# The maxima product of key tile 1 moved to the head of a pair's first slot, in a fused attention, MLP and soft-MoE kernel

## The chip, the cores and the metric

The kernel runs on one NeuronCore of a Trainium2 chip. The metric is the device time of one execution in microseconds (us). The engines are named as in the profile: PE is TensorE (matmuls; PEld is its weight load), DVE is VectorE, ACT is ScalarE, POOL is GpSimd, SP is SyncE, which issues the DMAs.

## The reference

```python
# q, k, v: (4 batches, 12 heads, 448, 64)
scores = scale * np.matmul(q, k.transpose(0, 1, 3, 2))   # causal mask: -1e9 above the diagonal
scores = scores - np.max(scores, axis=-1, keepdims=True)
attn = np.exp(scores)
attn = attn / (np.sum(attn, axis=-1, keepdims=True) + 1e-09)
x = np.matmul(attn, v)                       # heads joined: (1792, 768)
h = x @ w_in; x = np.maximum(0.01 * h, h) @ w_out        # 768 -> 2048 -> 768
logits = x @ phi                             # 32 slots, 4 for each of 8 experts
d = softmax(logits, axis=0); slot_input = d.T @ x
slot_out[e] = np.maximum(slot_input[e] @ w1[e], 0) @ w2[e]
out = softmax(logits, axis=1) @ slot_out
```

All inputs are float32 and the result is (1792, 768) float32.

## The kernel before

**Pairs and rounds.** Attention works on pairs of heads, 6 pairs for each of the 4 batches, 24 in all. The generator `attention_slots` issues their work in rounds. A round has three slots, each ended by a `yield`. The first loop (L553) serves the first batch. The second loop (L587) holds the rounds n = 7 to 24 and is the one that changes; "round n" below is its loop variable. A round works on three pairs at once: it finishes pair n-1, computes the weights of pair n, and the row maxima of pair n+1.

**Maxima.** A pair's 448 keys and queries are four tiles of 112. For a softmax the row maximum of the scores is wanted first. `maxima(n, tiles)` (L377) multiplies the high parts of q and k of a tile into a PSUM tile `S`, for both heads, and DVE reduces each half to a column of `mxe` (L396, shown as `junk<-S`, followed by a short read of the accumulator). The tiles come in three calls: `TILES[0]` is tile 3 (448 columns, S_3 below), `TILES[1]` tiles 0 and 2 (S_0), `TILES[2]` tile 1 (224 columns, S_1). `lowering(n)` (L402) transposes `mxe` on PE (`mps`), and ACT writes four rows `mr` from it.

**Weights.** `weights(n, g)` (L410) makes the transposed scores in a PSUM tile `T` by six matmuls from the stacks `qkt` and two that add `mr`; T_0, T_1, T_2 are its three calls. ACT takes the exponential into `P`, POOL masks the diagonal blocks (L436) and sums over key tiles into `tsum` (L441, L445).

**End of a pair.** `attend` (L451) multiplies P with v into `O`; `inverses` (L462) makes the row sums `dn`, which ACT copies to `rs` and DVE inverts in two halves (L474, 1.5 us each); `columns` (L486) multiplies O by `rs` and splits the result into two float16 halves, `x16`.

**What fills the slots.** In the rounds of the second loop `stage` (L803) puts a column block of the next product, H = x @ w_in (18 matmuls of 128x448 in float16), after most slots, and `prep_step` puts pieces of the conversion of w_in and w_out (the 64 bit pattern arithmetic on DVE and POOL, `cv`, `cs`, `raw`; w_ps, wt_ps, wp_ps, wf_ps on PE) between them. No H follows the slots 6 and 15 of a batch (`GAPS`), which are the first slots of rounds 9, 12, 15, 18 and 21, 24. H has one PSUM buffer.

**What sets the order.** `in_order` chains all of these matmuls, so PE takes them in the order in which they are written; ACT's order is chained in the same way from the second batch on. DVE's and POOL's order comes from the scheduler. S and T share one PSUM tag, "S", with two buffers of two banks each: a new S or T tile takes a buffer whose last reader (DVE's maxima or ACT's exponential) is done. Which of the two buffers it takes is settled when the program is built, by the scheduler's estimate of what is free first.

Of the kernel before, what the change touches and what calls it, by code (L numbers as in the profile page):

```python
# [34 lines left out]
def tile_attn_moe_softmoe(ctx: ExitStack, tc: tile.TileContext, q, k, v, w_in, w_out, phi, w1, w2, out, dbg=None):  # L35
# [292 lines left out]
    def load_qk(n):  # L328
        b, hp = divmod(n, NP)
        t = att.tile([CP, 2, 2 * NI * D], F32, tag="qk", bufs=2, name=f"qk{n}")  # L330
        t = t.rearrange("p j (c x) -> p j c x", c=NI)
        for j, src in enumerate((q, k)):
            for a in range(2):
                nc.sync.dma_start(
                    t[:, j, :, D * a : D * (a + 1)], src[b, 2 * hp + a].rearrange("(c p) d -> p c d", p=CP)
                )
        qk_t[n] = t
        loaded_last()
# [11 lines left out]
    def reduce_v(n):  # L350

        b, hp = divmod(n, NP)
        if hp == 0:
            v_am[b] = am = const.tile([128, NP + 1], F32, tag="v_am", bufs=2, name=f"v_am{b}")
            nc.vector.memset(am, 0.0)
        with tc.issue_after(last_on(mybir.EngineType.DVE)) if b else ExitStack():
            nc.vector.tensor_reduce(v_am[b][:CP, hp : hp + 1], v_t[n], AX.XY, ALU.max, apply_absolute_value=True)

    def v_scale(b):

        am = v_am[b]
        nc.vector.tensor_reduce(am[:, NP:], am[:, :NP], AX.X, ALU.max)
        s_v[b], inv_v[b] = pow2_scale(am[:, NP:], f"v{b}")

    def qk_stacks(n):

        t = qk_t.pop(n)
        st = att.tile([128, 2, 2, S], F32R, tag="qs", bufs=2, name=f"qkt{n}")
        for j in range(2):
            p = ps_tr(f"qkps{n}_{j}", (128, S))  # L370
            for c in range(NI):
                tr(p[:, CP * c : CP * (c + 1)], t[:, j, c], ident[:CP, :CP])
            scalar.copy(st[:, j, 0], p)
            nc.vector.tensor_tensor(st[:, j, 1], p, st[:, j, 0].bitcast(F32), ALU.subtract)  # L374
        st_t[n] = st

    def maxima(n, tiles):  # L377

        st = st_t[n]
        ps = psum.tile([CP, 2, 512], F32, tag="S", bufs=2, name=f"S{n}_{tiles[0]}")  # L380
        at = 0
        for i in tiles:
            w = CP * (i + 1)
            for a in range(2):
                r = slice(64 * a, 64 * a + 64)
                mm(
                    ps[:, a, at : at + w], st[r, 0, 0, CP * i : w], st[r, 1, 0, :w], start=True, stop=True,
                    skip_group_check=True,
                )
            at += w  # L390
        at = 0
        for i in tiles:
            w = CP * (i + 1)
            for a in range(2):
                junk = att.tile([CP, S], BF16, tag="junk", bufs=1, name=f"junk{n}_{i}_{a}")
                nc.vector.tensor_tensor_reduce(  # L396
                    out=junk[:, :w], in0=ps[:, a, at : at + w], in1=mask[:, S - w :], scale=-1.0, scalar=3e38,
                    op0=ALU.add, op1=ALU.min, accum_out=mxe[n % 2][:, 64 * a + i : 64 * a + i + 1],
                )
            at += w  # L400

    def lowering(n):  # L402

        ps = ps_tr(f"mps{n}", (128, CP))
        tr(ps, mxe[n % 2], ident[:CP, :CP])
        mr_t[n] = mr = att.tile([128, NI, CP], F32R, tag="mr", bufs=1, name=f"mr{n}")
        for i in range(NI):
            scalar.activation(mr[:, i], ps, AF.Copy, scale=own[:, i : i + 1])
# [42 lines left out]
    def attend(n):  # L451

        p, vt = pbuf[n % 2], v_t.pop(n)
        o_t[n] = o = psum.tile([128, S], F32, tag="O", name=f"O{n}")
        for j in range(NI):
            for a in range(2):
                mm(
                    o[64 * a : 64 * a + 64, CP * j :], vt[:, a * NI + j, :], p[j // 2][:CP, a, j % 2, : S - CP * j],
                    start=j == 0, stop=j == NI - 1, skip_group_check=True,
                )  # L460
# [80 lines left out]
    def attention_slots():  # L541


        for n in range(2):
            qk_stacks(n)
            load_qk(n + 2)
            if n == 0:
                for tiles in TILES:
                    maxima(0, tiles)
        for x in range(NP):  # L550
            reduce_v(x)
        v_scale(0)
        for n in range(NP + 1):  # L553
            here, more = n < NPAIR, n + 1 < NPAIR
            if n > 0:
                attend(n - 1)
            if here:
                lowering(n)
            if more:
                maxima(n + 1, TILES[0])  # L560
            if here:
                weights(n, 0)
            yield
            if n > 0:
                inverses(n - 1)
            if more:
                maxima(n + 1, TILES[1])
            if here:
                weights(n, 1)
            yield  # L570
            if n > 0:
                columns(n - 1)
            if here:
                weights(n, 2)
            if more:
                maxima(n + 1, TILES[2])
            if n + 2 < NPAIR:
                qk_stacks(n + 2)
                if n + 4 < NPAIR:
                    load_qk(n + 4)  # L580
            if n + NP < NPAIR:
                load_v(n + NP)
            if NP <= n + NP - 1 < NPAIR:
                reduce_v(n + NP - 1)
            yield

        for n in range(NP + 1, NPAIR + 1):  # L587
            here, more = n < NPAIR, n + 1 < NPAIR
            attend(n - 1)
            inverses(n - 1)  # L590
            if here:
                lowering(n)
            yield
            if more:
                maxima(n + 1, TILES[2])
            if here:
                weights(n, 0)
            if more:
                maxima(n + 1, TILES[0])
            if n % NP == 1 and n + NP - 2 < NPAIR:  # L600
                v_scale(n // NP)
            yield
            if here:
                weights(n, 1)
                weights(n, 2)
            if more:
                maxima(n + 1, TILES[1])
            if n + 2 < NPAIR:
                qk_stacks(n + 2)
                if n + 4 < NPAIR:  # L610
                    load_qk(n + 4)
            if n + NP < NPAIR:
                load_v(n + NP)
            columns(n - 1)
            if n + NP - 1 < NPAIR:
                reduce_v(n + NP - 1)
            yield

    TILES = ((3,), (0, 2), (1,))
    slots_of_attention = attention_slots()  # L620


# [490 lines left out]
```

## Time and profile before

| what | value |
|---|---|
| median of 3 runs | 681.62 us (679.66 to 689.91) |
| the profiled execution | 681.57 us, span 679.8 us |
| mean granted PE clock | 0.963 |
| busy over the span | PE 583.1 us (86%), DVE 362.9 us (53%), ACT 291.9 us (43%), POOL 235.1 us (35%) |
| rounds 7 to 24 | about 103 to 460 us of the span |

The span is the time from the first to the last instruction of the profiled execution; the 1.8 us beside it lie around the instructions. A busy share says how long an engine had work in it. Whether that work sets the time is seen from what the engines wait for: the profile gives, for an instruction, the idle time of its engine just before it and who ended that idle time. Matmuls are pipelined, so a row's duration on PE is longer than the distance to the next row's start.

### The profile page before, as it was taken

The page shows a single profiled execution, that of the slowest core. Times are in us where ns is not written, and L with a number is a line of the kernel's source. Part 1 is how long each engine was busy: PE and PEld are TensorE (multiplying, and loading weights), DVE is VectorE, ACT ScalarE, POOL GpSimd, SP SyncE. Part 2 cuts the span into 40 slices and gives each one's busy share as a digit, 9 for nine tenths or more (in the row PEclk, how much of TensorE's full clock was granted, in tenths as well). Part 3 has the DMA queues.
Part 4 walks back from the last instruction along what each step waited for, and adds up shares of the span by engine and source line. Part 5 has one row for each costly group of instructions (what it writes and reads, how often), then busy time and mean ns, then how long its engine had stood idle before and what let it go on. Part 6 is the DMA issues. An engine that isn't in the chain of part 4 may idle for free.

```text
span 679.8 us, 12302 instructions
## 1 busy us (share of the span) xinstructions
PE 583.1 (86%) x4836; PEld 329.7 (48%) x4836; DVE 362.9 (53%) x884; ACT 291.9 (43%) x571; POOL 235.1 (35%) x247
## 2 busy tenths in 40 slices
PE   3778888989998998999999989999889978997374
PEld 2555555545554555555556544554334434553124
DVE  5868567979855565555557556434664341001004
ACT  2577555767764656564455444531202121011003
POOL 4277862577774335533334422430000000000000
PEclk9999889999999999999999979999999997999958
DMA  9941345556622456543243313029966545999957
GB/s 186 275 110 45 79 133 156 168 161 169 195 70 71 151 179 202 162 132 80 65 127 107 101 40 99 22 65 324 336 279 277 185 171 239 423 425 423 426 216 324
DMA packets 102449, 125.67 MB, mean 185 GB/s; under 512 B 69240, under 2 KB 91256, under 8 KB 98296
## 3 DMA queue, kind: packets, MB, share of 16 engines
q1 hardware_dynamic: 102392, 124.89, 55.9%
q8 instruction: 38, 0.62, 0.4%
q14 instruction: 19, 0.16, 0.1%
HBM read 105.74 MB, written 19.14 MB: 184 GB/s over the span
## 4 chain that ended last, share of the span: by engine, by line
PE 54%; POOL 11%; DMA 11%; DVE 10%; ACT 6%; issue 4%; SPq 2%; ACTq 0%; DVEq 0%; POOLq 0%
PE H L102 25%; DMA w<-in_moe_w_dram 9%; PE O L102 4%; PE T L102 4%; PE g_acc L102 3%; DVE g_nat L632 3%; PE S L102 3%; DVE rs L474 2%; POOL w L245 2%; POOL tsum L445 2%; ACT P L113 2%; POOL tsum L441 2%; PE dn L102 2%; DMA raw_i_None<-in_moe_w_in_dram 2%; POOL P L436 2%
## 5 line engine op out<-in xcount | busy, mean ns | idle before, releaser
L102 PE MATMUL H<-x,w 128*128 128x448 f16 x1152 | 233.5, 357 | 0.7 <-ACT g L113 0.7
L102 PEld LDWEIGHTS <-w 128*128 128x128 f16 x1152 | 112.0, 100 | 112.4 <-issue 21.0
L396 DVE CUSTOM_DVE_ANT_0 junk<-S,mask 112x224 bf16<-112x224 f32 (+3 forms) x192 | 85.0, 443 | 65.0 <-PE S L102 62.1
L113 ACT ACTIVATE g<-H,iv 128x448 f32<-128x448 f32 x58 | 36.8, 635 | 119.8 <-PE H L102 91.4
L474 DVE RECIPROCAL rs<-rs 128x224 f32<-128x224 f32 x36 | 53.4, 1524 | 50.2 <-ACT rs L113 50.2
L113 ACT ACTIVATE P<-T 112x672 f32<-112x672 f32 (+1 forms) x72 | 57.1, 793 | 23.6 <-PE T L102 22.2
L436 POOL TENSOR_SCALAR_AFFINE_SELECT P<-P 112x448 f32<-112x448 f32 x48 | 29.4, 613 | 107.4 <-ACT P L113 76.9
L102 PE MATMUL T<-qkt 64*112 64x336 f32 (+3 forms) x576 | 58.3, 315 | 4.0 <-ACT P L113 3.4
L102 PE MATMUL O<-P,v 112*64 112x448 f32 (+3 forms) x384 | 52.8, 415 | 5.6 <-POOL P L436 4.4
L102 PE MATMUL S<-qkt 64*112 64x224 f32 (+3 forms) x192 | 33.4, 388 | 20.1 <-DVE mxe L396 12.3
L445 POOL TENSOR_TENSOR tsum<-tsum,P 112x448 f32<-112x448 f32 (+1 forms) x48 | 47.6, 993 | 1.9
L102 PEld LDWEIGHTS T<-qkt 64*112 64x112 f32 x576 | 43.1, 180 | 10.2 <-ACT P L113 3.7
L1059 PE MATMUL po<-w,hz 128*32 128x384 f32 x256 | 27.9, 558 | 18.7 <-DMA w<-in_moe_w_dram 18.7
L102 PEld LDWEIGHTS O<-P,v 112*64 112x64 f32 x384 | 25.8, 139 | 31.9 <-issue 14.1
L441 POOL TENSOR_TENSOR tsum<-P 112x672 f32<-112x672 f32 x24 | 39.9, 1663 | 1.9
L963 POOL MEMSET hz<- 128x256 f32 x2 | 0.6, 312 | 108.6 <-PE g_acc L102 108.6
L632 DVE STREAM_TRANSPOSE g_nat<-g 128x448 f32<-128x448 f32 x26 | 16.5, 640 | 34.2 <-ACT g L113 34.2
L374 DVE TENSOR_TENSOR qkt<-qkps,qkt 128x448 fp32r<-128x448 f32 x48 | 29.2, 621 | 9.8 <-ACT qkt L113 9.8
L102 PE MATMUL T<-mr,onesr 64*112 64x448 f32 (+1 forms) x192 | 30.5, 314 | 3.9 <-ACT mr L113 3.9
L102 PEld LDWEIGHTS S<-qkt 64*112 64x112 f32 x192 | 15.9, 182 | 35.1 <-DVE mxe L396 17.5
L113 ACT ACTIVATE mr<-mps,own 128x112 fp32r<-128x112 f32 x96 | 26.2, 361 | 14.5 <-PE mps L102 14.4
L236 POOL TENSOR_TENSOR cv_i_None<-cv_i_None,cs_i_None 128x768 f32<-128x768 f32 x16 | 28.6, 1785 | 11.1 <-ACT cs_i_None L113 11.1
(174 smaller groups left out, 866.8 us busy)
## 6 DMA issues: line engine op xcount, KB each, us to landing
w<-in_moe_w_dram SPq DMA_DIRECT2D x32, 1536.0 KB
raw_i_None<-in_moe_w_in_dram SPq DMA_DIRECT2D x16, 768.0 KB
raw_o_None<-in_moe_w_out_dram SPq DMA_DIRECT2D x10, 768.0 KB
g_far<-g SPq DMA_DIRECT2D x32, 224.0 KB
gb<-g_far SPq DMA_DIRECT2D x8, 896.0 KB
wo<-wsc SPq DMA_DIRECT2D x4, 1536.0 KB
qk<-in_q_dram SPq DMA_DIRECT2D x48, 112.0 KB
qk<-in_k_dram SPq DMA_DIRECT2D x48, 112.0 KB
```

Of the source, the lines that this page charges most:

```text
L102: op(*args, **kwargs)
L113: op(*args, **kwargs)
L236: nc.gpsimd.tensor_tensor(t, t, sg, ALU.mult)
L245: nc.gpsimd.tensor_tensor(lo, w, hi, ALU.subtract)
L374: nc.vector.tensor_tensor(st[:, j, 1], p, st[:, j, 0].bitcast(F32), ALU.subtract)
L396: nc.vector.tensor_tensor_reduce(out=junk[:, :w], in0=ps[:, a, at : at + w], in1=mask[:, S - w :], scale=-1.0, scalar=3e38, op0=ALU.add, o ...
L436: nc.gpsimd.affine_select(out=d, in_=d, compare_op=ALU.is_ge, fill=0.0, base=0, pattern=[[0, 4], [1, CP]], channel_multiplier=-1,)
L441: nc.gpsimd.tensor_tensor(tsum[:CP], p[0][:CP, :, 0, CP:], p[0][:CP, :, 1, : S - CP], ALU.add)
L445: nc.gpsimd.tensor_tensor(y, y, p[1][:CP, :, j, : S - CP * (j + 2)], ALU.add)
L474: nc.vector.reciprocal(rs[:, c : c + S // 2], rs[:, c : c + S // 2])
L632: nc.vector.transpose(g_nat[:, :, 32 * f : 32 * (f + n)].rearrange("p c (f x) -> p f c x", x=32), gts[b, f].rearrange("p (c x) -> p c x", ...
L1059: nc.tensor.matmul(po[h][32 * g : 32 * g + 32], hp[:, (t0 + t) % 8], wt[:, t, DH * h - c0 : DH * (h + 1) - c0], start=t0 + t < 4, stop=t0 ...
```

## The change

In the second loop the call `maxima(n + 1, TILES[2])` moves from the head of the second slot to the head of the first, in front of `attend(n - 1)`. It makes the same two matmuls and the same two DVE reductions, on the same data.

```diff
         for n in range(NP + 1, NPAIR + 1):
             here, more = n < NPAIR, n + 1 < NPAIR
+            if more:
+                maxima(n + 1, TILES[2])
             attend(n - 1)
             inverses(n - 1)
             if here:
                 lowering(n)
             yield
-            if more:
-                maxima(n + 1, TILES[2])
             if here:
                 weights(n, 0)
             if more:
```

On PE, in round 9, where no H stands between the two slots, the kernel before issues this. O, dn and mps are of the first slot, S_1 (the row of 112x224) heads the second, T_0 follows and then S_3, the last row.

```order
L102 MATMUL w_ps<-ident,w_am_1686 128x128
L102 MATMUL O_1838<-P_448_144,v_711 64x448 x2
L102 MATMUL O_1838<-P_448_144,v_711 64x336 x2
L102 MATMUL O_1838<-P_224_145,v_711 64x224 x2
L102 MATMUL O_1838<-P_224_145,v_711 64x112 x2
L102 MATMUL dn_1847<-P_448_144,onesr 64x112 x2
L102 MATMUL dn_1847<-tsum,onesr 64x336 x2
L102 MATMUL mps_1856<-ident,mxe_143 128x112
L102 MATMUL S_1_1877<-qkt_1775 112x224 x2
L102 MATMUL T_0_1884<-qkt_1516 112x448 x6
L102 MATMUL T_0_1884<-mr_1858,onesr 112x448 x2
L102 MATMUL S_3_1894<-qkt_1775 112x448 x2
```

The same place of the changed kernel:

```order
L102 MATMUL w_ps<-ident,w_am_1686 128x128
L102 MATMUL S_1_1838<-qkt_1775 112x224 x2
L102 MATMUL O_1845<-P_448_144,v_711 64x448 x2
L102 MATMUL O_1845<-P_448_144,v_711 64x336 x2
L102 MATMUL O_1845<-P_224_145,v_711 64x224 x2
L102 MATMUL O_1845<-P_224_145,v_711 64x112 x2
L102 MATMUL dn_1854<-P_448_144,onesr 64x112 x2
L102 MATMUL dn_1854<-tsum,onesr 64x336 x2
L102 MATMUL mps_1863<-ident,mxe_143 128x112
L102 MATMUL T_0_1884<-qkt_1516 112x448 x6
L102 MATMUL T_0_1884<-mr_1865,onesr 112x448 x2
L102 MATMUL S_3_1894<-qkt_1775 112x448 x2
```

S_1 has moved from between mps and T_0 to the head, so that O, dn, mps and T_0 now stand between it and S_3. In the rounds with an H it passes that H too. The other rows of PE keep their order.

On DVE, the same round before: the two maxima of S_1 are junk_1_0 and junk_1_1, RECIPROCAL is the inversion of `rs`, the last junk row is S_3's.

```order
L396 ISA junk_1_0_1880,mxe_142<-S_1_1877,mask 112x224
L396 ISA mxe_142 112x1
L474 RECIPROCAL rs_1852<-rs_1852 128x224 x2
L396 ISA junk_1_1_1882,mxe_142<-S_1_1877,mask 112x224
L396 ISA mxe_142 112x1
L507 SCALAR_TENSOR_TENSOR rs_1852<-O_1838,v_s,rs_1852 128x448
L357 TENSOR_REDUCE v_am_1542<-v_1795 112x1
L215 TENSOR_REDUCE w_am_1867<-cv_i_None 128x1
L396 ISA junk_3_0_1897,mxe_142<-S_3_1894,mask 112x448
L396 ISA mxe_142 112x1
```

And in the changed kernel, where the rows L130 to L137 are a piece of the weights' conversion:

```order
L396 ISA junk_1_0_1841,mxe_142<-S_1_1838,mask 112x224
L396 ISA mxe_142 112x1
L130 TENSOR_SCALAR w_m_1830<-w_m_1830 128x1
L396 ISA junk_1_1_1843,mxe_142<-S_1_1838,mask 112x224
L396 ISA mxe_142 112x1
L132 TENSOR_SCALAR w_e<-w_m_1830 128x1
L134 TENSOR_SCALAR w_s<-w_e 128x1
L137 TENSOR_SCALAR inv_w<-w_e 128x1
L474 RECIPROCAL rs_1859<-rs_1859 128x224 x2
L396 ISA junk_3_0_1897,mxe_142<-S_3_1894,mask 112x448
L396 ISA mxe_142 112x1
```

Both maxima of S_1 now stand in front of the reciprocals, which before stood between or ahead of them. ACT's instructions keep their order throughout; on POOL one conversion step (L245) of round 9 moves behind the last `tsum` step (L445) of that round, and its two maskings (L436) now follow each other.

## Rows read from the trace of the kernel before

**Rows 1.** The page, busy time of PE over the span

```profile
PE 583.1 (86%) x4836; PEld 329.7 (48%) x4836; DVE 362.9 (53%) x884; ACT 291.9 (43%) x571; POOL 235.1 (35%) x247
```

**Rows 2.** Stretches: us, then busy (instructions) of PE, PEld, DVE, ACT, POOL; clock; DMA

```profile
103.00:226.00 123.00, 111.28 (x784) 64.70 (x785) 91.19 (x225) 79.36 (x146) 72.83 (x60) 0.99 0.50 138
```

**Rows 3.** PE's groups, 103 to 460 us: count, busy, mean ns, idle before

```profile
L102 PE MATMUL S<-qkt 64*112 64x448 f32 x32 | 7.6, 470 | 14.7 <-DVE mxe L396 8.5 <-ACT P L113 6.1
L102 PE MATMUL T<-mr,onesr 64*112 64x448 f32 x34 | 6.4, 371 | 1.1 <-ACT mr L113 1.1
L102 PE MATMUL dn<-tsum,onesr 128*64 128x336 f32 x72 | 13.5, 452 | 2.8 <-POOL tsum L445 2.8
```

**Rows 4.** PE in time order, round 7: start us, us, instruction, idle before it

```profile
110.32 0.36 PE L102 MATMUL S<-qkt 64*112 64x224 f32 x2
110.52 0.77 PE L102 MATMUL T<-qkt 64*112 64x448 f32 x6
112.31 0.46 PE L102 MATMUL S<-qkt 64*112 64x448 f32 x2 [0.82 <-DVE mxe L396]
```

**Rows 5.** PE in time order, round 22

```profile
418.29 0.45 PE L102 MATMUL S<-qkt 64*112 64x448 f32 x2 [1.03 <-DVE mxe L396]
418.67 3.58 PE L102 MATMUL H<-x,w 128*128 128x448 f16 x18
```

**Rows 6.** ACT and PE in time order, round 8

```profile
131.31 0.92 ACT L113 ACTIVATE P<-T 112x896 f32<-112x896 f32 x1
132.28 0.46 PE L102 MATMUL S<-qkt 64*112 64x448 f32 x2 [1.01 <-ACT P L113]
```

**Rows 7.** All engines in time order, round 9

```profile
146.01 0.79 PE L102 MATMUL dn<-tsum,onesr 128*64 128x336 f32 x4 [0.63 <-POOL tsum L445]
146.90 0.53 ACT L113 COPY rs<-dn 128x448 f32<-128x448 f32 x1 [3.25 <-PE dn L102]
147.69 2.96 DVE L474 RECIPROCAL rs<-rs 128x224 f32<-128x224 f32 x2
150.56 0.33 DVE L396 CUSTOM_DVE_ANT_0 junk<-S,mask 112x224 bf16<-112x224 f32 x1
150.95 0.46 PE L102 MATMUL S<-qkt 64*112 64x448 f32 x2 [2.02 <-DVE mxe L396]
```

**Rows 8.** ACT in time order, round 9, the exponential of T_1

```profile
157.66 1.50 ACT L113 ACTIVATE P<-T 112x672 f32<-112x672 f32 x2 [0.34 <-PE T L102]
```

**Rows 9.** DVE, POOL and PE in time order, round 10

```profile
162.53 0.95 DVE L215 TENSOR_REDUCE w_am<-cv_i_None 128x1 f32<-128x768 f32 x1 [0.21 <-ACT cv_i_None L113]
163.59 2.61 DVE L216 TENSOR_SCALAR cv_i_None<-cv_i_None 128x768 int32<-128x768 int32 x1
177.40 0.61 DVE L396 CUSTOM_DVE_ANT_0 junk<-S,mask 112x448 bf16<-112x448 f32 x1
...
164.12 1.66 POOL L245 TENSOR_TENSOR w<-cv_i_None,w 128x768 f16<-128x768 f32 x1
...
178.36 0.47 PE L102 MATMUL T<-qkt 64*112 64x224 f32 x6
```

**Rows 10.** Stretches of PE: us, busy (instructions), granted clock, DMA share, GB/s

```profile
151.00:157.00 6.00, 6.00 (x24) 0.72 0.00 0
394.00:402.00 8.00, 7.08 (x26) 0.57 0.24 65
```

**Rows 11.** PE in time order, round 21

```profile
391.21 0.41 PE L102 MATMUL wf_ps<-istack,w 96*128 96x32 f32 x2 [0.44 <-ACT rs L113]
392.30 0.52 PE L102 MATMUL wt_ps<-ident,cv_o 128*128 128x128 f32 x3 [0.68 <-ACT wprime L113]
394.92 0.72 PE L102 MATMUL S<-qkt 64*112 64x448 f32 x2 [1.01 <-ACT P L113]
395.56 6.30 PE L102 MATMUL H<-x,w 128*128 128x448 f16 x18
```

**Rows 12.** Stretch of PE after the rounds, columns as in Rows 10

```profile
540.00:560.00 20.00, 15.81 (x87) 0.95 0.48 190
```

## The prediction

> **What bounds the kernel now.** First the busy shares: PE works 583.1 us of the span [rows 1], so PE comes first, and a change pays by taking idle time from PE or work from its queue. This change takes no work away; it can only move waits. So the next view is PE's groups with their idle time, over the 357 us of rounds 7 to 24. One group of the attention stands out: S_3, the product of key tile 3, has 14.7 us of idle time in front of it, put down to DVE's maxima (8.5) and to ACT's exponential (6.1) [rows 3]. That is 15 waits, one in each of the rounds 7 to 22 but round 14: the first 0.82, the last 1.03 us [rows 4, 5], eleven of them between 0.8 and 1.1, the longest 2.02 in round 9 [rows 7].
>
> The time order says why. S_1, T_0 and S_3 come directly after each other, and two buffers hold all three. Where S_3 takes S_1's buffer, it waits for DVE to reduce S_1: in round 9 DVE inverts `rs` in between (2.96 us), does S_1's second half only at 150.56, and S_3 starts at 150.95 [rows 7]. Where it takes T_0's, it waits for the exponential of T_0, which runs from 131.31 for 0.92 us, with S_3 at 132.28 [rows 6]. In both cases the next thing on PE is queued behind S_3, since PE's order is fixed. The wait is on the path, not beside it.
>
> **The change part by part.** *S_1 at the head.* The same two matmuls, about 0.20 us of PE (the next product starts 0.20 after S_1, though the row says 0.36) [rows 4]. They move within PE's queue, so this costs nothing by itself. What S_1 needs there is the high half of the stack, cast by ACT in the slot before, and a free buffer, that of T_2; from round 8 on an H of 3.58 us [rows 5] lies between those and S_1, and covers them. In round 7 no H does, but there O already waits for the same stack. Without that cover all of O, dn, mps and T_0 would be queued behind S_1; I take 0. No DMA is issued by the call, and SP's queue has only two loads a place earlier or later.
>
> *The wait of S_3.* S_1's maxima now have all of O, dn, mps and T_0 to be done in. In the built program S_3 takes S_1's buffer in all 16 rounds, so it no longer meets T_0's exponential either; that falls to T_1, behind a whole H. Removed: 14.7 us. A wait also exposes the end of the matmul before it, which is otherwise overlapped: 0.36 of duration less 0.20 of distance, 0.16 for each [rows 4], so 15 x 0.16 = 2.4 (between 0 and 2.4; I take all of it, as it is the same pair of rows). Sum 17.1.
>
> *Rounds 9 and 10.* Here another engine is close behind. DVE is busy 91.2 of 123 us in the first of the three batches [rows 2], and from the reciprocals at 147.69 to the last maximum of S_3 of round 10, which ends at 178.0, it has hardly a pause (the largest 0.21 us) [rows 7, 9]. T_2 of round 10 needs that maximum and starts at 178.36 [rows 9]. ACT leaves little room either: in front of the exponential of T_1 in round 9 it is idle for 0.34 us [rows 8], and before that its queue is nearly full back to the copy of `rs`, so that round can gain about 1 us and not 2.2. What can DVE give? The reciprocals start when `rs` is there, at 146.90 + 0.53 = 147.43, 0.26 earlier; S_1's second maximum (0.33 and a short read of 0.08) moves in front of them; two pauses of about 0.2 give 0.4; the slack of T_2 gives 0.2. That is 1.3 for the two rounds, instead of 2.02 + 1.01 + 2 x 0.16 = 3.35. Loss: 2.05. The masking order on POOL also removes a wait of dn in round 10, the largest part of the 2.8 us of that group [rows 3], which goes into the same 1.3.
>
> *Small terms.* In round 12 T_0 waits 0.5 for `mr` (two such waits, 1.1 in all, the other in round 9) [rows 3]; S_1 filled 0.2 of that time and no longer does: -0.2. In round 8 T_2 follows S_3's maxima closely, as in round 10: -0.2. In front of dn PE waits 2.8 us in all for `tsum` [rows 3]; in four of those waits outside round 10 S_1's 0.2 now runs in the waiting time: between 0 and +0.8, I take 0.4.
>
> So far: 17.1 - 2.05 - 0.4 + 0.4 = 15.05.
>
> *The clock.* In two stretches PE runs below its full 2.4 GHz: mean granted 0.72 over 151 to 157 and 0.57 over 394 to 402, where H takes 6.30 instead of 3.58 [rows 5, 10, 11]. Both begin at the end of an S_3 wait: 2.02 in round 9; in round 21 1.01, after 0.44 and 0.68 in the three us before [rows 7, 11]. A lone 1.03 in round 22 left H at 3.58 [rows 5]. With the 1.01 gone, round 21 keeps 1.12 of idle time, close to the lone one, so I expect its H at full clock: 6.30 - 3.58 = 2.7, between 0 and 2.7. In round 9 DVE and ACT set the pace, so a full clock gives nothing beyond the 1.3.
>
> The Trainium skill has a rule on this ("TensorE: Matmul & The Clock Gate", section "HAM oscillation — how this bites in real kernels"): short bursts between idle gaps make the clock fall again and again. The trace agrees twice, with 0.72 and 0.57. By that rule an idle time that is only moved can pull the clock down elsewhere, which is the second rival.
>
> **Sum.** 15.05 + 2.7 = 17.8 us off the profiled execution's 681.57, which is 0.05 from the median of the runs: 663.8 us. This carries to the end because what follows is set off by PE: the weights of the experts are loaded into buffers that H frees, and before that last stretch DMA is not full (0.48 over 540 to 560) [rows 12], so those loads move forward with it.
>
> **The rivals.** *The clock doesn't come back, or falls elsewhere.* In round 9 PE would be 2.2 us sooner by the wait and 1.7 by the clock (6 us at 0.72 instead of 1.00 [rows 10]), but ACT lets S_0 start only about 1 us sooner; so up to 2.9 us of idle time gather there, as long as the wait that pulled the clock down [rows 7, 8]. A fall costs between that 1.7 and 2.7. Without the 2.7: 666.5; with one or two falls more: up to 671.
>
> *DVE or ACT takes over in all of rounds 7 to 12.* For it: DVE's share there [rows 2], and that its steps stretch when POOL runs beside them: L216 took 2.61 us while POOL had L245 [rows 9]; against it: outside rounds 9 and 10 DVE has idle time in front of its reciprocals. The six rounds hold 6.8 of the 14.7 and 1.0 of the 2.4; if they give nothing, 17.1 - 7.8 = 9.3 is left: 672.3, or 669.6 with the clock back.
> The Trainium skill names the cause of such stretches ("GPSIMD Engine Reference", section "1. Specifications"): POOL shares its SBUF interfaces with DVE. The 2.61 agrees. It speaks against this change only where DVE paces, since nothing moves work off DVE.
>
> *The wait only changes its name.* T_1, T_2 or S_0 wait as long as S_3 did, or the last stretch is held by DMA anyway: 680 to 683. Against: an H separates S_3 from T_1 in every round.
>
> *Slower.* The one mechanism that could do it is the clock: if PE's idle time gathers in longer pieces in most rounds, each piece pulls it down and costs an H 1.7 to 2.7. With a gain of 15 this decides from the seventh extra fall on; ten of them give 681.6 - 15 + 22 = 689. Against: the total idle time shrinks, and only two of the 16 rounds fall now.
>
> **How the numbers follow.** Chances: forecast 0.50 (660 to 668), clock 0.23 (666 to 671), DVE 0.13 (669 to 675), name only 0.10, slower 0.04. The predicted time is that of the first, 663.8. The range of eight in ten runs from 660, where the small terms and dn's waits all come out well, to 674, which takes in the clock and most of the DVE case. About 2% is what a measurement of this kernel can tell from no change, here 668.0: faster holds the forecast and a good third of the clock case, 0.58; within 2% the rest of that, DVE and the change of name, 0.39; slower 0.03.
>
> **What would show it.** In the changed profile the idle time before S_3 should be under 2 us in place of 14.7. The sum is wrong in rounds 9 and 10 if they gain more than 2 us or nothing. A wait of S_0 for ACT in round 9 and a late T_2 in round 10 should appear. The stretch of round 21 should show clock 1.00 and an H of 3.6. Rounds 13 to 22 should each be shorter by about the S_3 wait they had, plus 0.16. The prediction fails if new idle time of over 8 us appears on PE in these rounds, if a slow clock appears in three or more of them, or if the rounds end some 15 us earlier and the execution does not.

## The result, and the profile after

| | median | runs | against before (95% interval) |
|---|---|---|---|
| before, beside the changed kernel | 683.84 us | 4 (679.66 to 689.91) | |
| changed | 665.22 us | 4 (664.25 to 667.12) | 0.9743 (0.9705 to 0.9781) |

The change makes the kernel 2.6% faster; the forecast was 663.8 us, the measured median is 665.22. By the ratio the gain is 17.5 us. The two medians differ by 18.6, but without the highest of the four runs of before (689.91) it would be 16.4. The profiled execution of the changed kernel took 664.25 us (span 662.3), 17.3 less than the one before. Among the runs of the experiments below, one of 934.55 us at a mean granted clock of 0.57 is left out of its median.

The page, busy times over the span:

```profile
PE 582.0 (88%) x4836; PEld 329.6 (50%) x4836; DVE 366.6 (55%) x884; ACT 291.4 (44%) x571; POOL 235.5 (36%) x247
```

PE works as long as before (582.0, before 583.1 [rows 1]) in a span that is 17.5 shorter: what went is idle time. DVE's instructions are the same 884, but they take 3.7 us more; that comes back below.

PE's groups from 102 to 460 us, columns as in [rows 3]:

```profile
L102 PE MATMUL dn<-tsum,onesr 128*64 128x336 f32 x72 | 13.4, 451 | 0.2 <-POOL tsum L445 0.2
...
L102 PE MATMUL S<-qkt 64*112 64x448 f32 x32 | 5.9, 363 | 0.0
L102 PE MATMUL S<-qkt 64*112 64x224 f32 x32 | 5.7, 353 | 1.2 <-DVE qkt L374 1.2
...
L102 PE MATMUL S<-qkt 64*112 64x112 f32 x32 | 4.8, 299 | 2.9 <-ACT P L113 2.1
...
L102 PE MATMUL w_ps<-ident,w_am 128*128 128x128 f32 x20 | 4.1, 288 | 1.4 <-DVE qkt L374 0.9 <-DVE w_am L215 0.5
```

The second row is the answer to the 14.7 us: S_3 waits for nothing any more. The wait before dn fell too, from 2.8 to 0.2 us. What is new adds up to about 4 us: 1.4 before w_ps (the last row, 0.0 before), 0.6 before an mps (below), and 2.9 before S_0 in place of 1.0 (the last row but one), 2.15 of it in one place. S_1's 1.2 is round 7's wait for the stack, which stood before O until now.

Rounds by their length, from one round's first O to the next one's on PE (us; 9+10 and 11+12 as sums):

| rounds | before | changed | gain | the forecast's share |
|---|---|---|---|---|
| 7 | 19.6 | 18.6 | 0.9 | 1.0 |
| 8 | 19.6 | 19.4 | 0.3 | 1.0 |
| 9+10 | 41.3 | 40.4 | 0.8 | 1.3 |
| 11+12 | 36.6 | 33.7 | 3.0 | 2.1 and a part of dn's 0.4 |
| 13 to 20, 22 | 188.0 | 180.2 | 7.8 | 8.2 and the rest of the 0.4 |
| 21 | 21.7 | 17.6 | 4.1 | 1.2 and the clock's 2.7 |
| sum of 7 to 23 | 346.0 | 329.2 | 16.9 | 17.8 |

The other 0.4 of the 17.3 us lies outside these rounds: the first of them began 1.0 us earlier in this execution, behind code that is unchanged, and what follows the last took 0.6 longer. So the gain of the rounds reaches the end of the execution, as the forecast had it.

PE in time order in round 21, the place of [rows 11]:

```profile
378.75 0.41 PE L102 MATMUL wf_ps<-istack,w 96*128 96x32 f32 x2 [0.44 <-ACT rs L113]
379.83 0.52 PE L102 MATMUL wt_ps<-ident,cv_o 128*128 128x128 f32 x3 [0.67 <-ACT wprime L113]
381.18 0.37 PE L102 MATMUL S<-qkt 64*112 64x448 f32 x2
381.48 3.58 PE L102 MATMUL H<-x,w 128*128 128x448 f16 x18
```

The two small waits ahead of S_3 are still there (0.44 and 0.67), its own 1.01 is gone, and H takes 3.58 instead of 6.30.

PE, ACT and DVE in time order, rounds 8 to 10, the places of [rows 6, 7, 9]:

```profile
135.93 2.26 DVE L217 SCALAR_TENSOR_TENSOR cv_i_None<-raw_i_None,cv_i_None 128x768 int32<-128x768 int32 x1
140.15 0.49 PE L102 MATMUL w_ps<-ident,w_am 128*128 128x128 f32 x2 [0.45 <-DVE qkt L374]
...
145.87 0.37 PE L102 MATMUL S<-qkt 64*112 64x448 f32 x2
150.22 0.46 PE L102 MATMUL w_ps<-ident,w_am 128*128 128x128 f32 x2 [0.47 <-DVE w_am L215]
153.60 1.34 ACT L113 ACTIVATE P<-T 112x672 f32<-112x672 f32 x2
154.38 0.61 PE L102 MATMUL S<-qkt 64*112 64x112 f32 x4 [2.15 <-ACT P L113]
154.91 1.75 PE L102 MATMUL qkps<-ident,qk 112*128 112x112 f32 x8
156.46 4.35 PE L102 MATMUL H<-x,w 128*128 128x448 f16 x18
...
164.70 0.31 PE L102 MATMUL mps<-ident,mxe 112*128 112x112 f32 x1 [0.58 <-DVE w_m L129]
```

S_3 of round 9 no longer waits its 2.02, but S_0 waits 2.15 for the exponential of T_1. Behind that wait qkps takes 1.75 and H 4.35 us. In rounds 8, 9 and 10 PE waits for DVE's conversion steps or what stands behind them (0.45, 0.47 and 0.58, and another 0.47 before w_ps in round 10). T_2 of round 10, which the forecast expected late, doesn't wait. Stretches of PE, columns as in [rows 10]:

```profile
152.00:156.00 4.00, 1.85 (x16) 0.83 0.21 46
156.00:160.00 4.00, 4.00 (x19) 0.74 1.03 348
378.00:385.00 7.00, 5.89 (x38) 1.00 0.03 12
```

The clock came back in round 21 (0.57 before) and fell in round 9 again, at a new place: the slow H is now the one behind S_0, no longer the one behind S_3.

### The profile page after: what moved, and what is told of

Its sections match the earlier page's. It is cut to its first block, busy times and chain, and to the rows that moved or that the text cites. A ratio compares the mean times of both kernels' runs of the same rounds, so it can differ in the third digit from the quotient of the medians.

```text
span 662.3 us, 12288 instructions
## 1 busy us (share of the span) xinstructions
PE 582.0 (88%) x4836; PEld 329.6 (50%) x4836; DVE 366.6 (55%) x884; ACT 291.4 (44%) x571; POOL 235.5 (36%) x247
## 4 chain that ended last, share of the span: by engine, by line
PE 60%; DMA 11%; DVE 10%; POOL 8%; ACT 6%; issue 3%; SPq 1%; ACTq 0%; POOLq 0%; DVEq 0%
PE H L102 26%; DMA w<-in_moe_w_dram 9%; PE O L102 5%; PE T L102 5%; PE g_acc L102 3%; PE dn L102 3%; PE S L102 2%; DVE g_nat L632 2%; PE qkps L102 2%; PE ph L971 2%; PE L L102 2%; DMA raw_i_None<-in_moe_w_in_dram 2%; PE wt_ps L102 2%; POOL w L245 2%; ACT P L113 2%
## 5 line engine op out<-in xcount | busy, mean ns | idle before, releaser
L102 PE MATMUL H<-x,w 128*128 128x448 f16 x1152 | 230.7, 355 | 0.7 <-ACT g L113 0.7
L102 PEld LDWEIGHTS <-w 128*128 128x128 f16 x1152 | 111.2, 99 | 112.4 <-issue 19.6
L436 POOL TENSOR_SCALAR_AFFINE_SELECT P<-P 112x448 f32<-112x448 f32 x48 | 31.0, 647 | 90.6 <-ACT P L113 53.6
L445 POOL TENSOR_TENSOR tsum<-tsum,P 112x448 f32<-112x448 f32 (+1 forms) x48 | 47.3, 986 | 1.9
L441 POOL TENSOR_TENSOR tsum<-P 112x672 f32<-112x672 f32 x24 | 39.1, 1630 | 1.8
L102 PE MATMUL S<-qkt 64*112 64x224 f32 (+3 forms) x192 | 31.5, 368 | 8.4 <-DVE mxe L396 3.7
L632 DVE STREAM_TRANSPOSE g_nat<-g 128x448 f32<-128x448 f32 x26 | 16.5, 638 | 30.2 <-ACT g L113 30.2
L236 POOL TENSOR_TENSOR cv_i_None<-cv_i_None,cs_i_None 128x768 f32<-128x768 f32 x16 | 28.6, 1785 | 11.0 <-ACT cs_i_None L113 11.0
L113 ACT COPY rs<-dn 128x448 f32<-128x448 f32 x18 | 9.6, 532 | 50.3 <-PE dn L102 50.3
```

What stands on the lines that cost most here:

```text
L102: op(*args, **kwargs)
L113: op(*args, **kwargs)
L236: nc.gpsimd.tensor_tensor(t, t, sg, ALU.mult)
L436: nc.gpsimd.affine_select(out=d, in_=d, compare_op=ALU.is_ge, fill=0.0, base=0, pattern=[[0, 4], [1, CP]], channel_multiplier=-1,)
L441: nc.gpsimd.tensor_tensor(tsum[:CP], p[0][:CP, :, 0, CP:], p[0][:CP, :, 1, : S - CP], ALU.add)
L445: nc.gpsimd.tensor_tensor(y, y, p[1][:CP, :, j, : S - CP * (j + 2)], ALU.add)
```

## Experiments

All ratios are to the kernel before, measured beside it.

**Which rounds pay.** Two kernels share the change between the first batch of the loop and the rest; in each the condition decides whether the call stands at the head of the first slot or of the second.

```diff
+            head = n < 13          # in the other kernel: n >= 13
+            if more and head:
+                maxima(n + 1, TILES[2])
             attend(n - 1)
...
-            if more:
+            if more and not head:
                 maxima(n + 1, TILES[2])
```

> S_1 heads the first slot in rounds 7 to 12 only; from round 13 on it stands where it stood before. Theory (the gain is the idle time in front of S_3, round by round, less what DVE and ACT hold back in rounds 8 to 10): these rounds give what they gave in the changed kernel, 5.0 us by the distances between its O products, so about 676.5 us against 681.6; the slow clock of round 21 stays. Rival (the rounds act on each other, and the gain comes from a shift of the whole chain): the sum of this kernel and of its counterpart, with the other rounds changed, is more than 2 us off the 16.8 us of all rounds together.

Measured: 676.44 us, 0.9904 (0.9863 to 0.9945). Rounds 7 to 12 give 4.6 us (forecast 5.0), and round 21 keeps its S_3 wait and its slow H (4.93). As the theory had it.

Up to round 12 this is the changed kernel's program, and so a second profile of its round 9, which comes out otherwise. PE, DVE and POOL in time order there:

```profile
154.36 1.66 POOL L245 TENSOR_TENSOR w<-cv_i_None,w 128x768 f16<-128x768 f32 x1 [0.94 <-ACT w L113]
154.37 2.06 DVE L216 TENSOR_SCALAR cv_i_None<-cv_i_None 128x768 int32<-128x768 int32 x1
158.22 0.50 PE L102 MATMUL S<-qkt 64*112 64x112 f32 x4 [2.13 <-ACT P L113]
159.48 3.57 PE L102 MATMUL H<-x,w 128*128 128x448 f16 x18
159.77 1.95 DVE L216 TENSOR_SCALAR cv_i_None<-cv_i_None 128x768 int32<-128x768 int32 x1
165.74 0.49 PE L102 MATMUL w_ps<-ident,w_am 128*128 128x128 f32 x2 [2.69 <-DVE qkt L374]
```

S_0 waits 2.13, as it does after the change, but the clock stays up (H 3.57). The round is not shorter for it: L216 took 2.06 and 1.95 us, where it took 0.56 and 0.89 in the changed kernel's profile, and w_ps waits 2.69 for the DVE step behind it. Round 9 takes 21.74 us, with the clock held, against 20.40 with the slow clock.

> S_1 heads the first slot from round 13 on only; rounds 7 to 12 are as before. Theory: 16.8 less 5.0, that is 11.8 us, about 669.8 us, with a full clock in round 21 (2.9 of the 11.8 us) and the two waits of 0.5 and 2.0 us in round 9 back. Rival (the clock in round 21 is an accident of the phase and not of the idle time in front of it): it falls again here, and the time is about 672.7 us.

Measured: 674.56 us, 0.9891 (0.9845 to 0.9937). Rounds 13 to 22 give the same 11.9 us as in the changed kernel, round 21 takes 17.6 and its H 3.58: the rival falls. But the time is 5 us above the forecast, and the trace says where half of it comes from: two rounds that were not touched were slower than before, round 9 by 1.3 and round 12 by 1.9 (round 10 was 0.7 faster). PE in time order in round 12 of this kernel:

```profile
211.57 0.46 PE L102 MATMUL S<-qkt 64*112 64x448 f32 x2 [1.01 <-ACT P L113]
211.96 5.26 PE L102 MATMUL H<-x,w 128*128 128x448 f16 x18
```

The wait in round 12 is the 1.02 us of before, in the same code; there H took 3.58 behind it, here 5.26. In this profile a wait of a microsecond cost 1.7 more than itself.

The rounds that the two kernels change give 4.6 and 11.9 us, together 16.5 of the 16.9 of the whole change. So nothing here speaks for the first experiment's rival, that the rounds act on each other. The run times can't tell: the two medians give 6.6 and 8.5 us, with intervals of about 3 us to either side.

**Is the wait one for a buffer?** S_1 stays at its old place, but is put into two of the banks that the transposes use, so that S_3 finds a free buffer.

```diff
-        ps = psum.tile([CP, 2, 512], F32, tag="S", bufs=2, ...)
+        if tiles == TILES[2] and n > NP + 1:
+            ps = [ps_tr(f"S{n}_1{a}") for a in range(2)]
```

> S_1 stays where it stood before, at the head of the second slot, but writes two banks of the tag tr (one per head) in place of a buffer of the tag S, so that S_3 finds a free buffer in every round. DVE still reduces S_1 around its reciprocals. Theory (the wait is one for a buffer): idle time in front of S_3 under 1 us, and 664 to 669 us; some new waits for tr banks in front of S_1 and of the small transposes. Rival (what pays is that S_1 and its maxima are done before O and the reciprocals): the wait goes, but another as long takes its place, at T_2 or at the next tr tile, and the time stays at 677 us or above.

Measured: 674.18 us, 0.9881 (0.9833 to 0.993). PE's groups from 102 to 460 us of this kernel:

```profile
L102 PE MATMUL S<-qkt 64*112 64x224 f32 x32 | 9.7, 355 | 8.4 <-DVE w_m L129 3.4 <-ACT wt L113 2.2 <-ACT mr L113 1.9
...
L102 PE MATMUL S<-qkt 64*112 64x448 f32 x32 | 7.3, 376 | 0.0
```

S_3 (the last row) has no wait, without a step of S_1 having moved in PE's order: the wait was one for a buffer. But S_1 now waits 8.4 us for its banks, behind readers of other transposes, and two H outside round 21 run slowly (4.53 and 4.89); the rounds give 8.7 us, half of the 16.9. T_2 of round 9 waits 2.12 for DVE's maxima, which it didn't before. So the time lies between the two forecasts: the theory is right on the cause of the wait, and other waits took half of the gain. Round 21, with no S_3 wait, runs at full clock here too.

**How far ahead must S_1 be?** It stands at the end of the first slot. An H, where there is one, then lies between S_1 and T_0, but O, dn and mps no longer do.

```diff
-            if more:
-                maxima(n + 1, TILES[2])
             attend(n - 1)
             inverses(n - 1)
             if here:
                 lowering(n)
+            if more:
+                maxima(n + 1, TILES[2])
             yield
```

(The lines with a minus are those of the changed kernel.)

> S_1 stands at the end of the first slot, behind the transpose of the maxima, and an H follows it in the rounds that have one there; in rounds 9, 12, 15, 18 and 21 it stands where it stood before. Theory: rounds with an H gain as in the changed kernel. Rounds 9 (2.0 us), 12 and 18 (1.0 each, for the exponential of T_0) keep their waits, 15 and 21 keep about half of them. So 17.1 - 2.2 - 1.2 - 1.2 - 1.0 = 11.5 us plus 2.7 if the clock of round 21 holds: 667 to 670 us. Rival (S_1 must stand in front of O, since otherwise its maxima stand behind the reciprocals): waits of 1 us in front of S_3 in most rounds, 677 us or above.

Measured: 672.18 us, 0.9854 (0.9812 to 0.9896). The rounds give 9.5 us. PE's group of S_3 from 102 to 460 us:

```profile
L102 PE MATMUL S<-qkt 64*112 64x448 f32 x32 | 6.8, 424 | 5.5 <-DVE mxe L396 3.5 <-ACT P L113 2.0
```

Rounds 12 and 18 give 0.0 and 0.1, as expected: no H lies there between S_1 and S_3. 5.5 us of S_3's waits are left, 2.03 of them in round 9 and 0.87 in round 21, where H takes 6.14 and 4.73; in the rounds with an H after the first slot S_3 waits for nothing. By the medians this kernel gains 10.9 us, a little under the 11.5 that the forecast had without the clock of round 21, which didn't hold. The rival falls: where an H lies between S_1 and T_0, S_1 need not stand in front of O. Where none does, only the place at the head has enough work behind it. By the profiles that place is worth 7 us more, the clock of rounds 9 and 21 included.

**Is it the wait that pulls the clock down in round 21?** The change without round 21, and round 21 alone:

```diff
+            head = n != 21         # in the other kernel: n == 21
+            if more and head:
...
+            if more and not head:
```

> The changed kernel with round 21 alone in the order of before. Theory (the S_3 wait of round 21 pulls the clock down): the wait is back with 1.0 us and H runs at 5 to 6.3 us instead of 3.58; round 21 takes 19.9 to 21.7 us instead of 17.6, and the execution 667.5 to 669.3 us instead of 665.2. Rival (the slow clock of round 21 in the profile of before was an accident of that execution): the wait is back, H stays at 3.6 us, round 21 takes 18.8 us, the execution 666.4 us.

Measured: 668.24 us, 0.9783 (0.9741 to 0.9824), 3.0 above the changed kernel (the profiled execution, 673.6, is the longest of the six; its round 7 also runs at a low clock). PE in time order, round 21:

```profile
390.06 0.71 PE L102 MATMUL S<-qkt 64*112 64x448 f32 x2 [1.01 <-ACT P L113]
390.71 4.70 PE L102 MATMUL H<-x,w 128*128 128x448 f16 x18
```

With the 1.01 the slow H is back; round 21 takes 20.35 us instead of 17.6, within the theory's 19.9 to 21.7.

> The kernel before with round 21 alone in the order of the change. Theory (the S_3 wait of round 21 pulls the clock down there): without the wait H runs in 3.58 us, round 21 takes 17.6 us instead of 21.66, and the execution about 4.1 us less than before: 678 to 680 us beside 682 to 683.5 of before. Rival (the clock of round 21 has another cause): round 21 takes 19.9 to 20.5 us and the execution is 1.2 us under before.

Measured: 682.04 us beside 684.00, 0.9959 (0.9926 to 0.9992). The interval holds both forecasts, 4.1 and 1.2 us; the trace tells them apart:

```profile
400.72 0.37 PE L102 MATMUL S<-qkt 64*112 64x448 f32 x2
401.02 3.58 PE L102 MATMUL H<-x,w 128*128 128x448 f16 x18
```

Round 21 takes 17.3 us instead of 21.7. In this profile the untouched rounds 7, 9, 12 and 18 are 1.1 to 1.7 us longer than in the one before (round 10 is 0.7 shorter), with an H of 6.13, 5.24 and 5.26 in the last three, so the profiled execution as a whole (683.48 us) gained nothing. Over all profiles in which round 21 has its old order of slots: with the S_3 wait its H was slow in four of four (6.30, 4.93, 4.73, 4.70); without it at full clock in nine of nine (the kernel with other slots without an H isn't counted).

**What paces rounds 8 to 10?** First DVE: L217, one step of the conversion, is left out.

```diff
-        nc.vector.scalar_tensor_tensor(ti, lw, 29, ti, ALU.logical_shift_right, ALU.bitwise_or)
+        if stage != 1 or kind != "i":
+            nc.vector.scalar_tensor_tensor(ti, lw, 29, ti, ALU.logical_shift_right, ALU.bitwise_or)
```

> The changed kernel without the step of DVE that joins the low word of the 64 bit pattern to the high one (L217) in the conversions of w_in that run in the rounds 7 to 18; the converted weights lose their low bits. It takes 1.0 to 2.3 us of DVE's time for each piece of weights, about 4.4 us of it in rounds 9 and 10. Theory A (DVE sets the pace in rounds 8 to 10, so the removed waits of S_3 gave only 1.1 us of the 4.7 there): these rounds get shorter by another 2 to 3.5 us, to 662 to 663 us in all. Theory B (ACT sets the pace there): the wait of S_0 for the exponential in round 9 stays at about 2 us and the execution at 664.5 to 665.5 us.

Measured: 662.22 us, 0.9691 (0.965 to 0.9733). The interval overlaps with that of the changed kernel; the rounds are clearer: 8 gives 0.7 more, 9 1.8 and 10 1.4. The waits of w_ps in round 8 and of mps and w_ps in round 10 are gone, so these two rounds were held back by DVE. (With the step left out the scheduler set DVE's other steps in another order, too, so the gain isn't the step's own time alone.) Round 9 is another matter. PE in time order there, and the stretch that follows:

```profile
154.81 0.51 PE L102 MATMUL S<-qkt 64*112 64x112 f32 x4 [2.14 <-ACT P L113]
155.25 0.99 PE L102 MATMUL qkps<-ident,qk 112*128 112x112 f32 x8
156.07 3.57 PE L102 MATMUL H<-x,w 128*128 128x448 f16 x18
```

```profile
155.00:159.00 4.00, 4.00 (x28) 1.00 0.98 287
```

S_0 waits as long as in the changed kernel, 2.14, yet the clock stays at 1.00: qkps takes 0.99 instead of 1.75, H 3.57 instead of 4.35. With S_0's own 0.1 that is 1.6 of the 1.8 us. Here neither DVE nor the clock holds PE behind S_0, and round 9 takes 18.6; with the change alone it had the one (20.40) or the other (21.74 in the first experiment). So theory A is right for rounds 8 and 10. For round 9 theory B has the wait of S_0, which is unchanged, and neither has what comes behind it. ACT in the changed kernel from the copy of `rs` to the exponential that S_0 waits for:

```profile
144.00:153.60 9.60, 9.44 (x16) 1.00 0.21 51
```

ACT has no pause there that the profile marks as a wait, and the stretch is 9.60 or 9.61 us in four profiles with the change (the changed kernel's, the first experiment's, that without round 21 and this one); before it was 10.76. Up to S_0 round 9 goes at ACT's pace.

Then ACT: L235, another step of the conversion, is left out, or is cut short.

```diff
-        scalar.activation(sg, sg, AF.Copy, scale=s_w)
+        if u[3] != 1:          # in the other kernel: on sg[:, :32] where u[3] == 1
+            scalar.activation(sg, sg, AF.Copy, scale=s_w)
```

> The changed kernel without the step of ACT that multiplies the signs by the scale (L235) in the conversions of w_in that run in the rounds 7 to 18; the converted weights are not scaled. It takes 0.95 us of ACT for each piece. Theory B (ACT's queue sets the pace in round 9): the exponential of T_1 comes 1 to 2 us sooner, the wait of S_0 for it falls from 2.15 us to under 1, with that the H of round 9 runs at full clock (3.58 instead of 4.35), and round 9 is 1 to 2.5 us shorter; the execution 662.5 to 664 us. Theory A (DVE sets the pace): the wait of S_0 gets shorter but T_2 or the products that wait for DVE get later by as much; round 9 and 10 together gain under 0.5 us.

Measured: 673.94 us, 0.9862 (0.9813 to 0.9911), 9 us slower than the changed kernel. The wait of S_0 falls to 0.70, as theory B had it, but another one takes its place in front of dn. PE in time order, rounds 9 and 10:

```profile
148.05 1.31 PE L102 MATMUL dn<-tsum,onesr 128*64 128x336 f32 x4 [2.83 <-POOL tsum L446]
157.93 0.51 PE L102 MATMUL S<-qkt 64*112 64x112 f32 x4 [0.70 <-ACT P L113]
172.67 1.39 PE L102 MATMUL dn<-tsum,onesr 128*64 128x336 f32 x4 [6.77 <-POOL tsum L446]
```

With the step gone the scheduler set POOL's order anew and put conversions in front of the sums that dn needs. So the time says nothing on ACT. The trace does: from the copy of `rs` to the exponential ACT takes 7.7 us instead of 9.60, shorter by the two steps that are gone there (0.97 and 0.93), and H behind S_0 runs at full clock (3.57).

> The changed kernel with the step of ACT that multiplies the signs by the scale (L235) cut to 32 of its 768 columns in the conversions of w_in that run in the rounds 7 to 18; the other columns stay unscaled. ACT has 0.7 us less work for each piece, and the step still stands in its queue, so that POOL's order is closer to that of the changed kernel than without the step. If ACT sets the pace in round 9: the wait of S_0 falls from 2.15 us to under 1.3, and round 9 is shorter by as much; in all 663 to 664.3 us. If DVE takes over at once: round 9 and 10 together within 0.5 us of the changed kernel's 40.4, in all 664.5 to 665.5 us.

Measured: 668.74 us, 0.9763 (0.9711 to 0.9815). POOL's order differs from the changed kernel's at fewer places, but dn still waits (6.0 us in all). ACT and PE in time order in round 9:

```profile
153.99 0.83 ACT L113 CAST w<-cv_i_None 128x768 f16<-128x768 f32 x1 [0.76 <-POOL cv_i_None L237]
158.17 0.51 PE L102 MATMUL S<-qkt 64*112 64x112 f32 x4 [2.12 <-ACT P L113]
```

Neither of its forecasts came: ACT has less to do, but waits 0.76 for POOL in front of the exponential, so the stretch from the copy of `rs` is only 0.6 shorter (9.02). PE reaches S_0 0.6 sooner after that copy, too, as w_ps no longer waits there, and S_0 waits 2.12 as before. So it is ACT's fixed queue, with conversion steps ahead of the exponential, that holds S_0 in round 9, and a shorter queue can run into POOL, which one of these steps needs. A kernel that gains by relieving ACT was not found: whether one can stays open.

**Three attempts at a faster kernel.** The slots without an H, and the pace at which conversions start:

```diff
-GAPS = (6, 15)
+GAPS = (12, 15)
```

> An attempt to beat the changed kernel: the slot without an H moves from the head of round 9 to the head of round 12 (and of round 15 to 18, 21 to 24), where fewer steps of the conversion run. An H of 3.6 us then stands between S_1 and T_0 in round 9. If the wait of S_0 in round 9 comes from the missing H, it goes (2.15 us) with the slow clock behind it (0.8): 662 us. If the columns of H are now needed before their weights are converted, PE waits for ACT or POOL in rounds 9 to 11 by 1 to 3 us a batch: 666 to 672 us.

(Slot 12 is the head of round 11, and of 17 and 23; the expectation says round 12 by mistake.) Measured: 666.06 us, 0.9754 (0.9701 to 0.9807). In round 9 the wait of S_0 is gone, as the first forecast had it, but H waits 0.80 there for ACT's read of the one before and dn 1.04 in round 10. Rounds 9+10 give 0.4 more; S_0 waits 1.49 for the exponential in round 11, where no H is now; the rounds sum to 329.1, as the changed kernel's 329.2.

```diff
-        last = slots - (6 if columns_of_g is not None and count <= NF else 4)
+        last = slots - (4 if columns_of_g is not None and count <= NF else 4)   # in the other kernel: 2
```

> An attempt to beat the changed kernel: its conversions of w_in in the rounds 7 to 12 are started over 14 slots instead of 12, so that each of the rounds 8 to 10 holds one seventh less of them. With DVE as the engine that sets the pace there, these rounds get 1 to 2 us shorter and the rounds 11 and 12 longer by under 1: 663.5 to 664.5 us. If DVE's steps are only stretched by POOL (L216 and L217 beside L245), the gain can be up to 3 us; if a column of H now waits for its weights, PE loses 1 to 3 us in rounds 10 to 12: 667.

Measured: 665.61 us, 0.9725 (0.9678 to 0.9772). Rounds 8 to 10 give 4.2 more, above the up to 3 expected, and rounds 11 and 12 lose it again, 0.9 and 3.3. PE in time order, round 12:

```profile
205.02 5.08 PE L102 MATMUL H<-x,w 128*128 128x448 f16 x17 [1.35 <-POOL w L245]
```

H waits 1.35 for its weights, the granted clock falls (0.91 over the round), and 17 of H's 18 matmuls take 5.08 us, where all 18 took 3.58.

> As the one before, with the conversions started over 16 slots: one quarter less of them in each of the rounds 8 to 10. If no H waits for its weights: 662 to 664 us. A wait for weights is likelier here, since the last conversion starts in slot 14 of 18 and its H stands in slot 17 or behind: 666 to 668 us then.

Measured: 696.25 us, 1.0167 (1.0117 to 1.0217): the wait for weights that was expected, but 20.6 us of it in front of H, where the forecast had put down about 4 us (666 to 668 instead of 662 to 664). None of the three is clearly faster than the changed kernel.

## Why the prediction was right, point by point

**Removed waits of S_3: as forecast.** 14.7 us in 15 places became nothing, and the kernel in which S_1 has banks of its own shows that they were waits for a buffer. Where nothing else is near, in rounds 13 to 20 and 22, the gain was 7.8. The waits there were 14.7 less the 6.8 of rounds 7 to 12 and the 1.0 of round 21 [rows 3, 11], so 6.9; that leaves 0.11 for each of the eight, where the forecast put 0.16 for the end that a wait exposes.

**The clock of round 21: right, 2.9 for 2.7.** Round 21 gave 4.06; 1.01 and 0.16 of that are the wait. The experiments that put the wait back and took it alone away moved the slow H with it. The size is partly luck: behind the same wait H took 6.30 in the profile of before, from which the forecast was made, and 4.70 to 4.93 in the three others, so the term lies between about 1.1 and 2.7, as its range had it, and the forecast used the upper end.

**Rounds 9 and 10: 0.84 for 1.3; only half of the reason was there.** The step was "in round 9 DVE and ACT set the pace, so a full clock gives nothing beyond the 1.3". The first experiment bears it out in part: with the clock held, DVE took over, and rounds 9 and 10 together were not shorter (41.1 us, the changed kernel 40.4). The profile after shows the other way. ACT's stretch from the copy of `rs` to the exponential got 1.2 us shorter, the forecast's "about 1 us"; but as dn of round 9 no longer waits its 0.63, the copy itself came 0.7 sooner, and S_0 starts 13.5 us behind the round's first O instead of 15.4. Behind S_0 the clock took 1.6 of these 1.8 us back: w_ps, S_1 and O of round 10 follow H without a wait, so the slow clock lay on the path. The rival "falls elsewhere" had the place (S_0 in round 9, up to 2.9 us of idle time; measured 2.15) and the price (1.7). Of the same program up to round 12 there are three profiles each: with S_1 at the head the two rounds take 40.4, 41.1 and 41.2 us, with the old order 41.3, 41.9 and 41.7. The gain is 0.7 on average. S_0 waited 2.12 to 2.16 in five profiles, and the clock fell in two of them (H 4.35 and 5.55); behind the old wait of S_3 (2.02 to 2.03) it fell in four of four (H 5.26 to 6.33).

**Round 8: -0.2 was too small.** It gave 0.3 instead of 1.0, and not for the forecast's reason: T_2, for which the -0.2 was put down, doesn't wait there. The second L217 of that round began 0.36 us behind POOL's sum (L441, at 135.57) and took 2.26 us. Before, it began 0.45 ahead of that sum (138.78) and took 1.18, while the sum took 2.20 instead of 1.80:

```profile
138.33 1.18 DVE L217 SCALAR_TENSOR_TENSOR cv_i_None<-raw_i_None,cv_i_None 128x768 int32<-128x768 int32 x1
```

In the changed kernel w_ps then waits 0.45 for what stands behind it on DVE. Without L217 the round gives 0.7 more. Over the rounds, DVE's group before and after:

```profile
L217 DVE SCALAR_TENSOR_TENSOR cv_i_None<-raw_i_None,cv_i_None 128x768 int32<-128x768 int32 x10 | 14.2, 1416 | 0.0
```

```profile
L217 DVE SCALAR_TENSOR_TENSOR cv_i_None<-raw_i_None,cv_i_None 128x768 int32<-128x768 int32 x10 | 16.5, 1649 | 0.1
```

The same ten instructions take 2.3 us more: in the faster kernel they stand otherwise beside POOL's work. The Trainium skill says this of the two engines ("GPSIMD Engine Reference", section "1. Specifications"): the SBUF interfaces are shared, with contention where DVE's instruction has two SBUF inputs, as L217 has. The trace agrees: in the changed kernel's profile L217 takes 0.96 us in round 7, where POOL does nothing beside it, and 2.28 in round 8 beside POOL's L245 and L236.

**dn: +0.4 was too small.** Its waits in rounds 11 and 12 (0.65 and 0.26 before) went entirely, those in 9 and 10 as well; the forecast gave each S_1's 0.2 at the most, and took half. Round 11 gave 1.69, which is 0.93 of S_3, 0.16 and the 0.65. These 0.5 us more make up for most of round 8.

**What the one profile of before didn't show.** The profiled execution of before took 681.57 us, while the 41 runs of before that were taken beside the experiments have a median of 683.7; against these the change gives 18.5 us. Round 12 shows one reason. Behind the same S_3 wait it took 16.85 us with H at 3.58 in the profile of before and in that of the fourth experiment, but 18.8 and 18.5 us with H at 5.26 and 5.24 in two others; with the change it took 15.3 to 15.6 in the six profiles with the same slots and pace. So the wait in round 12 was another place where the clock could fall, by chance, and the forecast gave no gain for it. In round 18 it fell in one of four such profiles (H 5.26).

**The rivals.** That DVE or ACT takes over in all of rounds 7 to 12 is refuted: they gave 5.0 of 7.8. That the wait only changes its name holds in round 9 alone (20.36 us before, 20.40 after). That the kernel gets slower is refuted. In total 17.3 us came for 17.8. That the sum is this close is in part luck: the misses on dn, on round 8 and on rounds 9 and 10 nearly cancel, and the clock's term was read from the profile with the slowest H.

## What to carry to other kernels

When a product waits for a rotating buffer, look at which earlier tile holds it and what lies between the two on the engine that has to read it; moving the holder ahead of work that doesn't need the buffer removed the wait here without new work, while a bank of its own only helps if nobody else uses it (here S_1 then waited 8.4 us for it). Price a wait on PE by the clock as well: a microsecond cost up to 2.9 us more here, and the wait that took its place in round 9 cost 1.6 in the same way. Where two engines are near the bound, expect a gain in one round to lengthen their instructions through contention, and judge by rounds, because terms of opposite sign hide in the total.

## What was not expected of the hardware

Whether PE's clock falls behind a wait differs between profiles of the same code and the same wait: in round 12 a wait of 1.01 or 1.02 left H at 3.58 in two profiles and went with 5.26 and 5.24 in two others; in round 9 a wait of 2.14 left the clock at 1.00, and 2.15 took it to 0.74. In round 21, where two shorter waits precede that of 0.9 to 1.0, it fell in four of four. For a single round the clock is therefore worth a range and not a number.

The contention of DVE and POOL also hangs on a hair. In the changed kernel's profile POOL's L245 of round 9 begins at 150.51 and DVE's L216 at 150.52; in that of the first experiment the two begin at 154.36 and 154.37. In the one DVE took 0.56 us and POOL 2.08, in the other DVE 2.06 and POOL 1.66.

```profile
150.51 2.08 POOL L245 TENSOR_TENSOR w<-cv_i_None,w 128x768 f16<-128x768 f32 x1 [0.94 <-ACT w L113]
150.52 0.56 DVE L216 TENSOR_SCALAR cv_i_None<-cv_i_None 128x768 int32<-128x768 int32 x1
```

A step of 0.56 us can thus cost 2.06 in another execution, although PE's, DVE's, ACT's and POOL's instructions up to there are the same and in the same order.
